# A new order for every step of a long-convolution and soft-MoE kernel on one core

## The chip, the cores and the metric

The kernel runs on one core of one Trainium2 chip, as a single launch. The metric is the time of that core on the device, in microseconds; lower is better. Everything is fp32.

## The reference

Two blocks stand behind each other. The first is a causal long convolution of 8 sequences of 5696 positions and 128 channels with one filter, written as a product of spectra:

```python
Xf = np.fft.rfft(x, n=2 * S, axis=1)
Hf = np.fft.rfft(h, n=2 * S, axis=0)
y = np.fft.irfft(Xf * Hf[None], n=2 * S, axis=1)[:, :S, :]
```

The second takes the 45568 rows of y as tokens of a soft mixture of experts with 32 slots (8 experts of 4):

```python
logits = x @ phi                        # 45568 x 32
d = softmax(logits, over the tokens)    # dispatch
c = softmax(logits, over the slots)     # combine
slot_in = d.T @ x                       # 32 x 128
slot_out[e] = relu(slot_in[e] @ w1[e]) @ w2[e]
out = c @ slot_out
```

So the dispatch needs all tokens before a slot is known, and the output needs the slots.

## The kernel before

The convolution is done as a transform in two factors, 90 x 64, with tables in place of an FFT's twiddles. The filter is group g = 0, the sequences are g = 1 to 8. One `while` loop over steps t (lines 430 to 504) carries everything; each step does one piece of four stages, and the order in which the loop body calls them is the order on each engine, since the schedule is manual.

- **A** (`stage_a`, line 158) transforms one chunk of 4 + 4 positions: `load_x` (135) fetches the low part xl and the mirrored high part xh by four DMAs, `fold` (149) makes their sum xe and difference xo on GpSimd (POOL), TensorE multiplies each with two tables (L165), ScalarE (ACT) copies the banks to fst (L167), and one DMA for each half writes f to HBM. Eight chunks make a group.
- **B** works on units of two frequency pairs, 23 units to a group, three to a step. `load_g` (176) reads gt from f by two DMAs. `stage_b1` (188): the forward product with wt (L195), then on VectorE (DVE) pr and pi, products with the filter's spectrum (L213), and yf, two combinations of them (L217, L219). `stage_b2` (223): the backward product with vt (L231), the copy zst (L234) and two DMAs to z. For the filter's own group DVE and ACT make Hr and Hi instead.
- **C** works on chunks again: `load_z` (248) reads zc; `stage_c1` (259) does four matmuls (L264), a copy yo, and a sum and a difference that are the tokens y (L270, L271); `stage_c2` transposes y (L281), `stage_c3` makes the logits L (L289), column and row maxima cm and rm, and the combine weights ct (POOL, ACT, then the row sums rs on DVE, L306 to L308, POOL again); `stage_c4` transposes ct (L318) and stores it as c_t.
- **Windows** of two chunks carry the running maximum of the dispatch softmax: `window_max` (328) makes c on DVE (L331), transposes it (L335) and reduces it, `window_row` (350) spreads it over the rows (L353) and makes d on POOL and ACT, `dispatch` (371) multiplies d with y into ap and sp (L382, L385), and DVE adds these to acc (L395).

A group's A takes steps 8g to 8g + 7; its B follows 9 steps behind, C 17 steps behind that. So there are steps with A alone, A and B, A and B and C, B and C, and C alone. Before the last stage the buffers of A and B are closed and the expert weights w1s and w2s loaded into their place (line 493). Behind the loop come the expert matmuls (L536, L541) and the output (L564), which multiplies each chunk of c_t with the slots and writes out by two DMAs for each half.

All matmul outputs take turns in six PSUM banks. Nearly all DMAs are issued by SyncE (SP), in the order of the code, and each waits there for its data. An fp32 matmul shows as two MATMUL in the profile.

Of the kernel before, what the change touches and what calls it, by code (L numbers as in the profile page):

```python
# [17 lines left out]
def transform_tables(S, N1, N2):  # L18

    N, R1, HALF = N1 * N2, S // N2, N2 // 2
    k1 = np.arange(N1)
    alpha = np.pi * (k1 + 0.5) / N1
    m1 = np.arange(R1) - (N1 - 1) / 2
    a1 = np.outer(m1, alpha)
    s1 = np.stack([np.cos(a1), -np.sin(a1), -np.cos(a1)], 1)
    i1 = np.stack([np.cos(a1.T), -np.sin(a1.T), -np.cos(a1.T)], 1)  # L30
# [22 lines left out]
def kernel(  # L53
# [44 lines left out]
    zd = [nc.dram_tensor(f"z_{b}", (N1, N2, 2, D), F32, kind="Internal").ap() for b in range(B)]  # L98
# [36 lines left out]
    def load_x(c):  # L135
        if c >= (B + 1) * NJ:
            return
        g, j = divmod(c, NJ)
        src = (h if g == 0 else x[g - 1]).rearrange("(a n) d -> a n d", n=N2)
        xl = apool.tile([R1, CH, D], F32, name="xl", tag="xl")  # L140
        xh = apool.tile([R1, CH, D], F32, name="xh", tag="xh")
        for t_, n0 in ((xl, CH * j), (xh, N2 - CH * (j + 1))):
            for r in (slice(0, SPLIT), slice(SPLIT, R1)):
                nc.sync.dma_start(out=t_[r, :, :], in_=src[r, n0:n0 + CH, :])
        xs[c] = (xl, xh)
# [3 lines left out]
    def fold(c):  # L149
        xl, xh = xs.pop(c)  # L150
        xe = apool.tile([R1, CH, D], F32, name="xe", tag="xe")
        xo = apool.tile([R1, CH, D], F32, name="xo", tag="xo")
        nc.gpsimd.tensor_tensor(out=xe[:, :, :], in0=xl[:, :, :], in1=xh[:, ::-1, :], op=AL.add)  # L153
        nc.gpsimd.tensor_tensor(out=xo[:, :, :], in0=xl[:, :, :], in1=xh[:, ::-1, :],
                                op=AL.subtract)
        folded[c] = (xe, xo)

    def stage_a(c, comp):
        g, j = divmod(c, NJ)
        src = folded[c][comp]  # L160
# [27 lines left out]
    def stage_b1(u):  # L188
# [8 lines left out]
        if g == 0:  # L197
            for q in range(n):
                m = 2 * i + q
                pr = bpool.tile([P, 2, D], F32, name="hp", tag="hp")  # L200
# [22 lines left out]
    def stage_b2(u):  # L223
# [20 lines left out]
    NYB = 5  # L244
# [3 lines left out]
    def load_z(c):  # L248
        if c >= B * NJ:
            return  # L250
        b, j = divmod(c, NJ)
        t_ = cpool.tile([N1, 2, CH, 2, D], F32, name="zc", tag="zc")
        v = zd[b].rearrange("k (o n) c d -> k o (n c d)", o=2)
# [31 lines left out]
    def stage_c3(c):  # L285
# [5 lines left out]
        L = ypool.tile([R1, 2 * CH, NSL], F32, name="L", tag="L", bufs=5)  # L291
# [12 lines left out]
        nc.scalar.activation(ct[:, :, :], ct[:, :, :], AF.Exp)  # L304
        rs = cpool.tile([R1, 2 * CH], F32, name="rs", tag="rs")
# [6 lines left out]
        cs[c] = ct  # L312
# [15 lines left out]
    def window_max(w):  # L328
# [4 lines left out]
                                in1=cm[:, 1:2, :].broadcast_to([R1, Q, NSL]), op=AL.max)  # L333
        p = bank()
# [65 lines left out]
    LAG_B, LAG_C = NJ + 1, 2 * (NJ + 1)  # L400
    PER = -(-NU // NJ)

    def units(t):
        s = t - LAG_B
        g, i = divmod(s, NJ)
        if s < 0 or g > B:
            return []
        return [g * NU + k for k in range(i * PER, min((i + 1) * PER, NU))]

    nc.sync.dma_start(out=s1[:, :, :], in_=t_s1)  # L410
    load_x(0)
# [3 lines left out]
    for p0 in range(0, NP, 9):  # L415
        nc.scalar.dma_start(out=wt[:, p0:p0 + 9, :], in_=t_w[:, p0:p0 + 9, :])
    for p0 in range(0, NP, 9):
        nc.scalar.dma_start(out=vt[:, p0:p0 + 9, :], in_=t_v[:, p0:p0 + 9, :])
    NA, NC = (B + 1) * NJ, B * NJ
    AHEAD = 3  # L420
    queue = [u for t in range(NA + LAG_C + NC) for u in units(t)]
    loaded = 0

    def c_first(t):
        c = t - LAG_C - NJ
        return c if 0 <= c < NC else None

    last_front = max(t for t in range(NA + LAG_C + NC) if units(t))
    t = 0
    while t <= NC + LAG_C + NJ + WC:  # L430
        a = t if t < NA else None
        us = units(t)
        c = c_first(t)
        cp = c_first(t - 1)
        if a is not None:
            load_x(a + 1)
            fold(a)
        if us or units(t + 1):
            pos = queue.index(us[-1]) + 1 if us else 0
            ahead = min(len(queue), pos + AHEAD)  # L440
        else:
            pos = ahead = 0
        nxt = c_first(t + 1)
        if nxt is not None:
            load_z(nxt)

        def want(u):
            nonlocal loaded
            k = min(len(queue), queue.index(u) + 1 + AHEAD)
            while loaded < k and queue[loaded] // NU * NJ + NJ <= t:  # L450
                load_g(queue[loaded])
                loaded += 1

        def b1(k):
            if k < len(us):
                stage_b1(us[k])

        def b2(k):
            if k < len(us):
                stage_b2(us[k])  # L460

        if not us and units(t + 1):
            want(units(t + 1)[0])
        for u in us:
            want(u)
        if a is not None:
            stage_a(a, 0)
        w_row = (c_first(t - WC) or 0) // WC if c_first(t - WC) is not None and c_first(t - WC) % WC == 0 else None
        if c is not None:
            stage_c1(c)  # L470
        if w_row is not None:
            window_row(w_row)
        b1(0)
        if a is not None:
            stage_a(a, 1)
            folded.pop(a)
        if c is not None:
            stage_c2(c)
        b2(0)
        b1(1)  # L480
        if c is not None:
            stage_c3(c)
        dc = c_first(t - WC)
        if dc is not None:
            dispatch(dc)
        b2(1)
        b1(2)
        if cp is not None:
            stage_c4(cp)
        if c is not None and c % WC == WC - 1:  # L490
            window_max(c // WC)
        b2(2)
        if t == last_front:
# [8 lines left out]
            hTz = wts.tile([P, E, NFC, NSL], F32, name="hTz")  # L502
            nc.gpsimd.memset(hTz[:, :, :, :], 0.0)
        t += 1
    assert not (ys or Ls or ds or cs or prods or gs or zs)
# [25 lines left out]
    sop = aps.tile([P, 512], F32, name="ap", tag="ap")  # L531
    for e in range(E):
# [5 lines left out]
        nc.scalar.activation(hTz[:, e, :, e * SPE:(e + 1) * SPE], hv, AF.Relu)  # L538
    for e in range(E):
        for k in range(NFC):  # L540
            nc.tensor.matmul(sop[0:NSL, 0:D], hTz[:, e, k, :], w2s[:, e, k, :],  # L541
                             start=(e == 0 and k == 0), stop=(e == E - 1 and k == NFC - 1))
    so = tail.tile([NSL, D], F32, name="so")
    nc.vector.tensor_copy(out=so[:, :], in_=sop[0:NSL, 0:D])
# [15 lines left out]
    for c in range(B * NJ):  # L560
        b, j = divmod(c, NJ)
        for f in range(2):
# [4 lines left out]
            o_ = osp.tile([R1, CH, D], F32, name="o", tag="o")  # L567
            pv = p[0:R1, :].rearrange("p (n d) -> p n d", d=D)
            if f:
                nc.vector.tensor_copy(out=o_[:, :, :], in_=pv)  # L570
            else:
                nc.scalar.activation(o_[:, :, :], pv, AF.Copy)
            n0 = N2 - CH * (j + 1) if f else CH * j
            for r in (slice(0, SPLIT), slice(SPLIT, R1)):
                nc.sync.dma_start(out=ov[b, r, n0:n0 + CH, :], in_=o_[r, :, :])
# [29 lines left out]
```

## Time and profile before

| | |
|---|---|
| median of 3 runs | 2017.19 us (2013.24 to 2018.6) |
| the profiled execution | 2011.97 us, of it 2010.2 us span |
| TensorE matmul busy | 1671.1 us, 83% |
| DVE, ACT, POOL busy | 753.0, 525.4, 308.6 us |
| mean granted TensorE clock | 0.788 |
| DMA | 277.60 MB, 138 GB/s |

The profile is of one execution. A row of a timeline gives start, length, engine, line, operation, output and inputs, count, and in brackets the idle time ahead of it and what ended it. "PE" is TensorE, "PEld" its weight loads, "SPq" the DMA issues on SP. The granted clock is the share of TensorE's full clock that its throttle let through.

### The profile page before, as it was taken

The numbers are of one execution on the slowest core, as the hardware profiler recorded it, in microseconds if no ns is written. First come the engines' busy times: TensorE is split into PE (matmuls) and PEld (weight loads), VectorE is DVE, ScalarE is ACT, GpSimd is POOL, SyncE is SP. The second block draws the span as 40 slices with busy tenths as digits, with TensorE's granted clock in tenths as the row PEclk, the third lists the DMA queues.
The fourth block names the chain that finished last, engine by engine and source line by source line (L and its number), as shares of the span: only waits on it lengthen the run. The fifth ranks groups of instructions, "written<-read, shape, count | busy, mean of one in ns | idle before, by whom it ended". The sixth has DMA issues, their size and how long they took to land.

```text
span 2010.2 us, 18430 instructions
## 1 busy us (share of the span) xinstructions
PE 1671.1 (83%) x5407; PEld 922.1 (46%) x5407; DVE 753.0 (37%) x1705; ACT 525.4 (26%) x1118; POOL 308.6 (15%) x345
## 2 busy tenths in 40 slices
PE   6986677888888888888888898889878884888999
PEld 2343334444444444444444444444445552445733
DVE  0143434443444344434444434343444531221133
ACT  2462222222222222222222222222221220111133
POOL 2321111111111111111112111111110110110000
PEclk9996878777887788778878878787887875555799
DMA  6675556555555455555555555555453446113166
GB/s 225 187 228 147 153 132 172 139 133 131 141 140 132 129 143 140 132 129 144 140 130 140 142 133 133 136 143 133 125 131 92 108 101 185 40 48 122 49 210 208
DMA packets 204438, 277.60 MB, mean 138 GB/s; under 512 B 24304, under 2 KB 139939, under 8 KB 204339
## 3 DMA queue, kind: packets, MB, share of 16 engines
q1 hardware_dynamic: 202506, 270.36, 50.1%
q10 hardware_dynamic: 1833, 6.06, 0.8%
q8 instruction: 45, 0.74, 0.2%
q14 instruction: 54, 0.44, 0.1%
HBM read 146.89 MB, written 129.43 MB: 137 GB/s over the span
## 4 chain that ended last, share of the span: by engine, by line
PE 66%; DVE 22%; DMA 3%; SPq 3%; POOL 2%; issue 2%; ACT 1%; POOLq 0%; ACTq 0%; DVEq 0%
PE bank L264 18%; PE bank L165 14%; PE bank L231 9%; PE bank L195 8%; PE bank L564 5%; PE ap L382 4%; DVE pr L213 4%; DVE pi L213 4%; DVE yf L217 4%; DVE yf L219 3%; PE bank L289 3%; DVE acc L395 2%; PE bank L536 1%; PE bank L281 1%; POOL ct L301 1%
## 5 line engine op out<-in xcount | busy, mean ns | idle before, releaser
L264 PE MATMUL bank<-zc,i 90*89 90x512 f32 x512 | 384.7, 921 | 21.5 <-DMA zc<-z 21.5
L231 PE MATMUL bank<-yf,vt 128*128 128x256 f32 x720 | 228.1, 444 | 138.6 <-DVE yf L219 138.5
L270 DVE TENSOR_TENSOR y<-bank,yo 89x512 f32<-89x512 f32 x64 | 43.9, 686 | 592.6 <-PE bank L264 541.9
L195 PE MATMUL bank<-gt,wt 128*128 128x256 f32 x810 | 255.3, 446 | 0.0
L165 PE MATMUL bank<-xe,s 89*90 89x512 f32 x288 | 218.4, 903 | 40.6 <-POOL xe L153 40.4
L167 ACT ACTIVATE fst<-bank 90x512 f32<-90x512 f32 x288 | 167.3, 592 | 306.4 <-PE bank L165 259.6
L264 PEld LDWEIGHTS bank<-zc,i 90*89 90x89 f32 x512 | 120.9, 238 | 256.6 <-issue 249.2
L213 DVE TENSOR_TENSOR pr<-bank,Hr 128x512 f32<-128x512 f32 (+1 forms) x184 | 124.4, 676 | 254.6 <-PE bank L195 254.5
L231 PEld LDWEIGHTS bank<-yf,vt 128*128 128x128 f32 x720 | 138.9, 215 | 176.1 <-issue 124.6
L195 PEld LDWEIGHTS bank<-gt,wt 128*128 128x128 f32 x810 | 182.3, 229 | 67.9 <-issue 36.0
L234 ACT ACTIVATE zst<-bank 128x512 f32<-128x512 f32 (+1 forms) x184 | 108.1, 588 | 374.9 <-PE bank L231 329.4
L165 PE MATMUL bank<-xo,s 89*90 89x512 f32 x288 | 177.6, 750 | 0.0
L382 PE MATMUL ap<-y,d 89*128 89x512 f32 x256 | 164.9, 735 | 1.5 <-ACT d L366 1.5
L301 POOL TENSOR_TENSOR ct<-L,rm 89x256 f32<-89x256 f32 x64 | 39.2, 612 | 776.1 <-DVE rm L299 776.1
L153 POOL TENSOR_TENSOR xe<-xl,xh 89x512 f32<-89x512 f32 x72 | 90.7, 1259 | 231.1 <-DMA xh<-in_x_dram 180.9
L213 DVE TENSOR_TENSOR pi<-bank,Hi 128x512 f32<-128x512 f32 (+1 forms) x184 | 123.0, 669 | 0.0
L165 PEld LDWEIGHTS bank<-xe,s 89*90 89x90 f32 x288 | 61.7, 220 | 130.4 <-issue 64.2
L564 PE MATMUL bank<-sobd,cT 128*89 128x512 f32 x256 | 111.8, 600 | 2.5 <-DVE sobd L555 2.5
L289 PEld LDWEIGHTS bank<-phi,yt 128*89 128x89 f32 x1024 | 104.0, 179 | 13.3 <-ACT yt L282 7.8
L363 POOL TENSOR_TENSOR d<-L,mr 89x256 f32<-89x256 f32 x64 | 45.1, 724 | 422.5 <-DVE mr L355 422.5
L289 PE MATMUL bank<-phi,yt 128*89 128x32 f32 x1024 | 102.3, 257 | 5.8 <-ACT yt L282 5.8
L335 PE MATMUL bank<-ident,c 89*128 89x89 f32 x32 | 11.0, 342 | 111.3 <-DVE c L331 111.3
(74 smaller groups left out, 1445.4 us busy)
## 6 DMA issues: line engine op xcount, KB each, us to landing
f<-fst SPq DMA_DIRECT2D x144, 360.0 KB, 3.6
gt<-f SPq DMA_DIRECT2D x396, 128.0 KB, 5.0
zc<-z SPq DMA_DIRECT2D x64, 720.0 KB, 6.3
z<-zst SPq DMA_DIRECT2D x352, 128.0 KB, 2.5
out_dram<-o SPq DMA_DIRECT2D x128, 160.0 KB, 2.2
xl<-in_x_dram SPq DMA_DIRECT2D x64, 160.0 KB, 2.5
xh<-in_x_dram SPq DMA_DIRECT2D x64, 160.0 KB, 2.5
c_t<-cst SPq DMA_DIRECT2D x64, 89.0 KB, 1.6
```

The lines of the kernel that those rows point to most:

```text
L153: nc.gpsimd.tensor_tensor(out=xe[:, :, :], in0=xl[:, :, :], in1=xh[:, ::-1, :], op=AL.add)
L165: nc.tensor.matmul(p[0:N1, :], s1[:, tab[G], :], src[:, :, :].rearrange("p n d -> p (n d)"), start=True, stop=True)
L167: nc.scalar.activation(st[:, :, G, :], p[0:N1, :].rearrange("p (n d) -> p n d", d=D), AF.Copy)
L195: nc.tensor.matmul(p[:, q * 256:(q + 1) * 256], wt[:, 2 * i + q, :], t_[:, q, :, :].rearrange("p c d -> p (c d)"), start=True, stop=True)
L213: nc.vector.tensor_tensor(out=t[:, 0:n, :, :], in0=pv[:, 0:n, :, :], in1=H[:, 2 * i:2 * i + n, :].unsqueeze(2).broadcast_to([P, n, 2, D]), ...
L217: nc.vector.tensor_tensor(out=y_[:, 0:n, 0, :], in0=pr[:, 0:n, 0, :], in1=pi[:, 0:n, 1, :], op=AL.subtract)
L231: nc.tensor.matmul(p[:, q * 256:(q + 1) * 256], vt[:, 2 * i + q, :], y_[:, q, :, :].rearrange("p c d -> p (c d)"), start=True, stop=True)
L234: nc.scalar.activation(st[:, 0:n, :], p[:, 0:n * 256].rearrange("p (q c) -> p q c", q=n), AF.Copy)
L264: nc.tensor.matmul(p[0:R1, :], i1[:, tabs[q], :], t_[:, o, :, q, :], start=(q == 0), stop=(q == 1))
L289: nc.tensor.matmul(p[0:R1, i * NSL:(i + 1) * NSL], yt[:, i, :], phi[:, :], start=True, stop=True)
L382: nc.tensor.matmul(ap_[:, :], dv, y_[:, f * CH:(f + 1) * CH, :].rearrange("p n d -> p (n d)"), start=first, stop=last)
L564: nc.tensor.matmul(p[0:R1, :], cT[:, c, f, :], sobd[:, f, :, :].rearrange("p q d -> p (q d)"), start=True, stop=True)
```

## The change

The stages are the same but for the three below; their order and their distance are new. A `for` loop takes the place of the `while` loop:

```diff
+        def slot_b():
+            nonlocal loaded
+            if us:
+                u = us.pop(0)
+                while loaded < len(queue) and queue[loaded][0] <= u + AHEAD \
+                        and queue[loaded][0] // NU * NJ + NJ <= t:
+                    load_g(queue[loaded][0])
+                    loaded += 1
+                stage_b1(u)
+                wait_b2.append(u)
+                if len(wait_b2) > 1:
+                    stage_b2(wait_b2.pop(0))
+            elif wait_b2:
+                stage_b2(wait_b2.pop(0))
...
+        c = chunk(0)
+        if chunk(-1) is not None:
+            load_z(chunk(-1))
+        if t < NA:
+            load_x(t + 3)
+            stage_a(t, 0)
+            fold(t + 1, 0)
+        r = chunk(3)
+        if r is not None and r % WC == 0:
+            window_row(r // WC)
+        slot_b()
+        c1 = chunk(1)
+        if c1 is not None:
+            stage_c2(c1)
         if c is not None:
             stage_c1(c)
...
+        slot_b()
+        if c1 is not None:
+            stage_c3(c1)
+        if t < NA:
+            stage_a(t, 1)
+            fold(t + 1, 1)
+        slot_b()
+        if c1 is not None:
+            stage_c3b(c1)
+            if c1 % WC == WC - 1:
+                window_max(c1 // WC)
+        if chunk(2) is not None:
+            stage_c4(chunk(2))
+        if c1 is not None and c1 % WC == WC - 1:
+            window_top(c1 // WC)
+        if r is not None:
+            dispatch(r)
```

`chunk(lag)` is the chunk whose C1 was `lag` steps ago: C1 stands at 0, C2 and C3 at 1, C4 at 2, the window's row and the dispatch at 3. `stage_c3b` is the second part of the old `stage_c3`, from the row sums rs on; `window_top` is the old `window_max` from its transpose on. In a slot the forward product of unit u stands ahead of the backward product of unit u - 1. `AHEAD` goes from 3 to 4 units, x is loaded three chunks ahead in one tile xc of three buffers, and folded one chunk ahead. The buffers of y and of L go from 5 to 4.

Three kinds of transfers are merged. Both parts of x come by one access pattern (two DMAs for four), z is stored by one DMA for a unit (two before; its layout in HBM changes, and the rows of the table i1 with it), and the two halves of an output chunk share their DMAs (two for four):

```diff
+        t_ = apool.tile([R1, 2, CH, D], F32, name="xc", tag="xc", bufs=3)
...
-        for par in range(2):
-            k0 = par * NP + 2 * i
-            nc.sync.dma_start(
-                out=zd[g - 1][k0:k0 + n, :, :, :].rearrange("k r c d -> r k (c d)"),
-                in_=st[par * N2:(par + 1) * N2, 0:n, :])
+        nc.sync.dma_start(
+            out=zd[g - 1][2 * i:2 * i + n, :, :, :].rearrange("q r c d -> r q (c d)"),
+            in_=st[:, 0:n, :])
```

The tables wt and vt were loaded by ACT's queue at the start; now SP loads a seventh of wt in each of steps 2 to 8, and of vt in each of steps 9 to 15. The expert weights are loaded one step later. The second expert product takes w2s as the stationary operand:

```diff
-            nc.tensor.matmul(sop[0:NSL, 0:D], hTz[:, e, k, :], w2s[:, e, k, :],
-                             start=(e == 0 and k == 0), stop=(e == E - 1 and k == NFC - 1))
+            for e in range(e0, e0 + 4):
+                nc.tensor.matmul(pp[e - e0][:, 0:SPE], w2s[:, e, k, :], hT[:, e, k, :],
+                                 start=(k == 0), stop=(k == NFC - 1))
```

and a transpose (with 8 small copies on DVE) turns the slots back.

What stands on the engines, in a step with A, B and C that ends a window. TensorE before, from the third stage of a chunk to the first of the next (phi: C3; ap and sp: dispatch; ct: C4; c: the window's transpose; gt and yf: B; xe and s: A; zc: C1):

```order
L289 MATMUL bank<-phi,yt 89x32 x8
L382 MATMUL ap<-y_100,d 128x512
L385 MATMUL sp<-ones,d 128x1
L382 MATMUL ap<-y_100,d 128x512
L385 MATMUL sp<-ones,d 128x1
L231 MATMUL bank<-yf,vt 128x256 x2
L195 MATMUL bank<-gt,wt 128x256 x2
L318 MATMUL bank<-ident,ct 128x89 x2
L335 MATMUL bank<-ident,c_4743 128x89
L231 MATMUL bank<-yf,vt 128x256 x2
L165 MATMUL bank<-xe,s_92 90x512 x2
L264 MATMUL bank<-zc,i_68 89x512 x4
```

And TensorE after, from C1 on (x_4447: the second half of A):

```order
L265 MATMUL bank<-zc,i_68 89x512 x4
L198 MATMUL bank<-gt,wt 128x256 x2
L234 MATMUL bank<-yf,vt 128x256 x2
L290 MATMUL bank<-phi,yt 89x32 x8
L168 MATMUL bank<-x_4447,s_92 90x512 x2
L198 MATMUL bank<-gt,wt 128x256 x2
L234 MATMUL bank<-yf,vt 128x256 x2
L322 MATMUL bank<-ident,ct 128x89 x2
L343 MATMUL bank<-ident,c_4612 128x89
L390 MATMUL ap<-y_99,d 128x512
L393 MATMUL sp<-ones,d 128x1
```

A forward and a backward product, of different units, now stand side by side; the dispatch went behind the window's transpose, and the second half of A between C3 and the third slot.

DVE before, ahead of the window's c:

```order
L296 TENSOR_REDUCE cm_104<-L 89x32
L299 TENSOR_REDUCE rm<-L 89x8
L306 TENSOR_REDUCE rs<-ct 89x8
L307 TENSOR_SCALAR rs<-rs 89x8
L308 RECIPROCAL rs<-rs 89x8
L395 SCALAR_TENSOR_TENSOR acc<-acc,dn,ap 32x128 x4
L395 SCALAR_TENSOR_TENSOR acc<-acc,dn,sp 128x1
L213 TENSOR_TENSOR pr<-bank,Hr 128x512
L213 TENSOR_TENSOR pi<-bank,Hi 128x512
L217 TENSOR_TENSOR yf<-pr,pi 128x2x128
L219 TENSOR_TENSOR yf<-pr,pi 128x2x128
L331 TENSOR_TENSOR c_4743<-cm_104 89x128
```

DVE after, at the same place:

```order
L297 TENSOR_REDUCE cm_103<-L 89x32
L300 TENSOR_REDUCE rm<-L 89x8
L216 TENSOR_TENSOR pr<-bank,Hr 128x512
L216 TENSOR_TENSOR pi<-bank,Hi 128x512
L220 TENSOR_TENSOR yf<-pr,pi 128x2x128
L222 TENSOR_TENSOR yf<-pr,pi 128x2x128
L311 TENSOR_REDUCE rs<-ct 89x8
L312 TENSOR_SCALAR rs<-rs 89x8
L313 RECIPROCAL rs<-rs 89x8
L335 TENSOR_TENSOR c_4612<-cm_103 89x128
```

The third unit's products and the row sums have changed places, both still ahead of c; the sums into acc went behind it.

SP before, one step of DMA issues:

```order
L255 DMA zc<-z 90x2x1024
L183 DMA gt<-f 64x512 x6
L170 DMA f<-fst 90x4x256 x2
L238 DMA z<-zst 64x2x256 x4
L323 DMA c_t<-cst 128x178
L238 DMA z<-zst 64x2x256 x2
L144 DMA xl<-in_x_dram 80x512
L144 DMA xl<-in_x_dram 9x512
L144 DMA xh<-in_x_dram 80x512
L144 DMA xh<-in_x_dram 9x512
```

SP after, the same:

```order
L256 DMA zc<-z 90x2x1024
L147 DMA xc<-in_x_dram 80x2x512
L147 DMA xc<-in_x_dram 9x2x512
L173 DMA f<-fst 90x4x256
L186 DMA gt<-f 64x512 x2
L239 DMA z<-zst 128x2x256
L186 DMA gt<-f 64x512 x2
L239 DMA z<-zst 128x2x256
L173 DMA f<-fst 90x4x256
L186 DMA gt<-f 64x512 x2
L239 DMA z<-zst 128x2x256
L327 DMA c_t<-cst 128x178
```

The 20 issues of a step are 15, and the reads of gt stand between the writes of f and z.

More of the change, by code (lines that the diff above doesn't have):

```diff
@@ L29, in transform_tables @@
     s1 = np.stack([np.cos(a1), -np.sin(a1), -np.cos(a1)], 1)
-    i1 = np.stack([np.cos(a1.T), -np.sin(a1.T), -np.cos(a1.T)], 1)
+    rows = np.arange(N1).reshape(2, N1 // 2).T.reshape(-1)
+    i1 = np.stack([np.cos(a1.T), -np.sin(a1.T), -np.cos(a1.T)], 1)[rows]
     k2 = np.arange(N2)
@@ L97 @@
     fd = [nc.dram_tensor(f"f_{g}", (N2, N1, 2, D), F32, kind="Internal").ap() for g in range(B + 1)]
-    zd = [nc.dram_tensor(f"z_{b}", (N1, N2, 2, D), F32, kind="Internal").ap() for b in range(B)]
+    zd = [nc.dram_tensor(f"z_{b}", (NP, 2 * N2, 2, D), F32, kind="Internal").ap() for b in range(B)]
     cd = nc.dram_tensor("c_t", (P, B * NJ, 2, R1), F32, kind="Internal").ap()
@@ L333, in window_max, with window_top @@
                                 in1=cm[:, 1:2, :].broadcast_to([R1, Q, NSL]), op=AL.max)
+        mrows[w] = c4
+    def window_top(w):
+        c4 = mrows[w]
         p = bank()
@@ L397, in dispatch @@
                                                op0=AL.mult, op1=AL.add)
-    LAG_B, LAG_C = NJ + 1, 2 * (NJ + 1)
+    LAG_B, LAG_C = NJ + 1, 3 * NJ + 2
     PER = -(-NU // NJ)
+    NA, NC = (B + 1) * NJ, B * NJ
     def units(t):
-        s = t - LAG_B
-        g, i = divmod(s, NJ)
-        if s < 0 or g > B:
+        g, i = divmod(t - LAG_B, NJ)
+        if t < LAG_B or g > B:
             return []
         return [g * NU + k for k in range(i * PER, min((i + 1) * PER, NU))]
+    steps = NC + LAG_C + WC + 2
+    queue = [(u, t) for t in range(steps) for u in units(t)]
+    last_front = queue[-1][1] + 1
+    AHEAD = 4
+    loaded = 0
     nc.sync.dma_start(out=s1[:, :, :], in_=t_s1)
-    load_x(0)
+    for c in range(3):
+        load_x(c)
     nc.scalar.dma_start(out=phi[:, :], in_=moe_phi)
@@ L414 @@
     nc.scalar.dma_start(out=i1[:, :, :], in_=t_i1)
[L415 to L447, printed above, removed]
-            nonlocal loaded
[L449 to L468, printed above, removed]
@@ new lines, with chunk @@
+    for comp in range(2):
+        fold(0, comp)
+    wait_b2 = []
+    for t in range(steps):
+        us = list(units(t))
+        def chunk(lag):
+            c = t - LAG_C - lag
+            return c if 0 <= c < NC else None
+        def slot_b():
+            nonlocal loaded
+            if us:
[10 more added lines that the diff above has]
+                stage_b2(wait_b2.pop(0))
+        if t < NJ + 1 and t >= 2:
+            p0 = NP * (t - 2) // (NJ - 1)
+            p1 = NP * (t - 1) // (NJ - 1)
+            nc.sync.dma_start(out=wt[:, p0:p1, :], in_=t_w[:, p0:p1, :])
+        if NJ + 1 <= t < 2 * NJ:
+            p0 = NP * (t - NJ - 1) // (NJ - 1)
+            p1 = NP * (t - NJ) // (NJ - 1)
+            nc.sync.dma_start(out=vt[:, p0:p1, :], in_=t_v[:, p0:p1, :])
+        c = chunk(0)
[12 more added lines that the diff above has]
+            stage_c2(c1)
@@ L469 @@
         if c is not None:
             stage_c1(c)
[L471 to L489, printed above, removed]
@@ L501 @@
                                   in_=moe_w2[e].rearrange("(c p) d -> p c d", p=P))
[L502 to L505, printed above, removed]
+    assert not (ys or Ls or ds or cs or prods or gs or zs or xs or folded or wait_b2)
     tail = work.enter_context(tc.tile_pool(name="tail", bufs=1))
@@ L537 @@
                              siT[:, e * SPE:(e + 1) * SPE], start=True, stop=True)
-        nc.scalar.activation(hTz[:, e, :, e * SPE:(e + 1) * SPE], hv, AF.Relu)
-    for e in range(E):
+        nc.scalar.activation(hT[:, e, :, :], hv, AF.Relu)
+    soT = tail.tile([P, NSL], F32, name="soT")
+    for e0 in range(0, E, 4):
+        pp = [bank() for _ in range(4)]
         for k in range(NFC):
-            nc.tensor.matmul(sop[0:NSL, 0:D], hTz[:, e, k, :], w2s[:, e, k, :],
-                             start=(e == 0 and k == 0), stop=(e == E - 1 and k == NFC - 1))
+            for e in range(e0, e0 + 4):
+                nc.tensor.matmul(pp[e - e0][:, 0:SPE], w2s[:, e, k, :], hT[:, e, k, :],
+                                 start=(k == 0), stop=(k == NFC - 1))
+        for e in range(e0, e0 + 4):
+            nc.vector.tensor_copy(out=soT[:, e * SPE:(e + 1) * SPE], in_=pp[e - e0][:, 0:SPE])
+    p = bank()
+    nc.tensor.transpose(p[0:NSL, 0:D], soT[:, :], ident[:, :])
     so = tail.tile([NSL, D], F32, name="so")
-    nc.vector.tensor_copy(out=so[:, :], in_=sop[0:NSL, 0:D])
+    nc.vector.tensor_copy(out=so[:, :], in_=p[0:NSL, 0:D])
     rep2 = tail.tile([NSL, Q, NSL], F32, name="rep2")
```

63 lines of the change are left out of this document (33 added, 30 removed).

## Prediction

> **What bounds the kernel now.** I read the page first, then the waits of TensorE, then a table by stage, then the timeline of single steps. In this page PE is TensorE's matmuls, and PEclk is the clock that the throttle granted in each fortieth of the span, in tenths:
>
> ```profile
> span 2010.2 us, 18430 instructions
> ...
> PE 1671.1 (83%) x5407; PEld 922.1 (46%) x5407; DVE 753.0 (37%) x1705; ACT 525.4 (26%) x1118; POOL 308.6 (15%) x345
> ...
> PEclk9996878777887788778878878787887875555799
> ```
>
> TensorE is busy for 83% of the span, no other engine for half of it, so the time is TensorE's. But its clock is rarely whole: a good part of the 1671 us is slow work, not much work. The same by stage (0 to 12 is the first load); the columns are busy time of each engine, then PEclk, the busy share of the DMA engines, GB/s:
>
> ```profile
> 12.00:80.00 68.00, 62.69 (x72) 18.72 (x72) 0.00 (x0) 21.40 (x36) 22.41 (x19) 1.00 0.66 212
> 80.00:145.00 65.00, 55.07 (x155) 29.40 (x155) 26.18 (x88) 41.58 (x121) 20.24 (x18) 0.95 0.77 227
> 145.00:307.00 162.00, 113.10 (x275) 62.45 (x276) 65.13 (x106) 36.42 (x64) 24.77 (x19) 0.77 0.56 152
> 307.00:1461.00 1154.00, 980.50 (x3395) 549.70 (x3394) 487.58 (x1099) 315.57 (x657) 200.65 (x226) 0.80 0.53 137
> 1461.00:1650.00 189.00, 156.13 (x583) 100.18 (x582) 85.69 (x209) 41.53 (x93) 18.06 (x28) 0.78 0.44 105
> 1650.00:1846.00 196.00, 147.55 (x417) 77.85 (x415) 42.58 (x130) 28.38 (x72) 20.73 (x30) 0.53 0.32 90
> 1846.00:1894.00 48.00, 44.38 (x260) 43.16 (x261) 1.96 (x10) 2.65 (x12) 0.00 (x0) 0.67 0.19 78
> 1894.00:2010.00 116.00, 111.69 (x256) 40.65 (x256) 43.92 (x64) 37.90 (x64) 0.00 (x0) 0.98 0.65 202
> ```
>
> I call them stages 1 to 8: A alone; A with the filter's B; A and B (9 steps); A, B and C (46 steps, 25.1 us each); B and C (9 steps); C alone; the expert matmuls; the output. Stage 4 decides. What TensorE waits for, over the whole trace (us, times, longest):
>
> ```profile
> PE bank L231 <- DVE yf L219: 138.5, 71, 4.5
> PE bank L335 <- DVE c L331: 111.3, 32, 4.6
> PE bank L165 <- POOL xe L153: 40.4, 14, 12.4
> PE bank L264 <- DMA zc<-z: 21.5, 1, 21.5
> ```
>
> So two waits on DVE matter: the backward product on its products yf, and the window's transpose on c. Here is one step of stage 4 on TensorE (start, us, and in brackets the idle time before it), and one group from the step ahead of it:
>
> ```profile
> 1112.66 7.03 PE L264 MATMUL bank<-zc,i 90*89 90x512 f32 x8
> ...
> 1135.78 1.10 PE L231 MATMUL bank<-yf,vt 128*128 128x256 f32 x4 [3.52 <-DVE yf L219]
> 1136.72 1.88 PE L165 MATMUL bank<-xe,s 89*90 89x512 f32 x4
> 1138.44 3.60 PE L264 MATMUL bank<-zc,i 90*89 90x512 f32 x8
> 1141.87 1.03 PE L195 MATMUL bank<-gt,wt 128*128 128x256 f32 x4
> 1142.74 1.88 PE L165 MATMUL bank<-xo,s 89*90 89x512 f32 x4
> ...
> 1147.36 1.38 PE L289 MATMUL bank<-phi,yt 128*89 128x32 f32 x16
> 1148.58 1.10 PE L382 MATMUL ap<-y,d 89*128 89x512 f32 x2
> ...
> 1152.55 0.32 PE L318 MATMUL bank<-ident,ct 89*128 89x89 f32 x2
> 1156.75 0.27 PE L335 MATMUL bank<-ident,c 89*128 89x89 f32 x1 [3.88 <-DVE c L331]
> 1156.85 1.06 PE L231 MATMUL bank<-yf,vt 128*128 128x256 f32 x4
> ```
>
> The same eight L264 take 7.03 us in one step and 3.60 in the next: half clock and whole. A gap therefore costs twice, once as idle time and once as the slow work behind it. When the clock falls and when it comes back (columns: TensorE busy, PEclk, DMA):
>
> ```profile
> 1134.00:1137.40 3.40, 1.62 (x6) 1.00 0.24 57
> 1154.50:1157.90 3.40, 1.15 (x6) 1.00 0.27 64
> 1157.90:1161.30 3.40, 3.40 (x6) 0.50 0.40 85
> ...
> 1663.00:1878.00 215.00, 169.20 (x519) 103.55 (x520) 38.99 (x122) 26.83 (x72) 17.71 (x27) 0.50 0.28 85
> ```
>
> A stretch of 3.4 us with 1.62 us of matmul kept the clock, one with 1.15 lost it. And in stage 6, with 169 of 215 us busy, it stayed at 0.50 throughout: there the dense matmuls feed 89 or 90 rows (L264, L382). In stage 8, whose L564 feeds 128 rows, it is 0.98. So I take it that the clock falls after about 3.4 us less than some 40% busy, and returns after about 3.4 us that are dense and hold some 128-row work (L195, L231).
>
> **The change part by part.**
>
> *Stage 4, the dense work.* No matmul is added or taken away. From 1136.72 to the end of L318 (1152.55 + 0.2) are 16.0 us at whole clock, without the third L231 group, which stands behind the gap: 0.94 (1135.78 to 1136.72). Sum 16.9, with a short wait in it and three units, where a chunk has 23 in eight steps. The other way: 980.5 us x 0.80 = 784, / 46 = 17.05. I take 16.8, 773 us for 46 steps.
>
> DVE in that same step:
>
> ```profile
> 1142.14 0.69 DVE L270 TENSOR_TENSOR y<-bank,yo 89x512 f32<-89x512 f32 x1 [6.51 <-PE bank L264]
> ...
> 1143.35 0.68 DVE L213 TENSOR_TENSOR pr<-bank,Hr 128x512 f32<-128x512 f32 x1
> ...
> 1145.00 0.42 DVE L219 TENSOR_TENSOR yf<-pr,pi 128x256 f32<-128x256 f32 x1
> ...
> 1151.74 0.42 DVE L306 TENSOR_REDUCE rs<-ct 89x8 f32<-89x256 f32 x1 [1.26 <-ACT ct L304]
> ...
> 1152.39 0.20 DVE L308 RECIPROCAL rs<-rs 89x8 f32<-89x8 f32 x1
> ...
> 1156.33 0.28 DVE L331 TENSOR_TENSOR c<-cm 89x128 f32<-89x128 f32 x1
> ```
>
> *The waits on yf go.* A unit's products take DVE 2.07 us (1143.35 to 1145.42). Now the backward product of unit u stands behind the forward one of u+1, and between the two slots lie C2 and C1, or C3 and A, or the dispatch and A: at least 1.22 + 1.72 us (starts of L289 and L382; of L165 and L264). With the 0.87 us of L195 (1141.87 to 1142.74) and 0.94 of L231 that is 4.7 us from the end of a unit's L195 to its L231, against 2.07 plus what stands ahead on DVE, at most the two y (1.21). Nothing for the wait is left. The other end is that a wait of today's mean length, 138.5 / 71 = 2.0 us, comes back in each step; it is kept for the range.
>
> *The wait on c stays, shorter.* In the new order c stands on DVE behind the third unit and the row sums. Count from the end of C1 (T = 1141.87 here). TensorE: two groups of B, 1.81; C3 1.22; A 1.72; two groups of B, 1.81; two transposes 0.2: it is at the window's transpose at T + 6.75. DVE: the third forward product ends at T + 5.6, its products start 0.27 later (as y does behind C1, 1142.14 - 1141.87) and end at T + 7.95; the three rs take 0.85 (1151.74 to 1152.59); from the start of c to L335 were 0.42. That is T + 9.2. The gap is 2.4 us in every second step, against 111.3 / 32 = 3.5 now. Bounds: 1.6 if the row sums come ahead of the products in time, 3.5 as now.
>
> *What the clock then does.* A stretch of 3.4 us around a gap of 2.4 is under 1.15 us busy when it holds nearly all of the gap, and over 1.62 when it holds less than about 1.8: between half and five sixths of the gaps should drop the clock. Behind the gap come the dispatch (1148.58 to 1152.55 less the two B groups in it, 2.16 us) and A (1.72), no 128-row work, then B, which restores it: some 8 us at half, 4 lost. I take 3.0 us for a gap on average (1.5 to 4).
>
> *Sum of stage 4:* 773 + 23 x 2.4 + 23 x 3.0 + 0.2 a step for the rest = 906 us, so -248. The DMA engines move the same bytes: 0.53 x 1154 = 612 us of their time, a share of 0.68, and stage 2 shows 0.77. SP gets fewer issues (15 for 20 in a step). Behind SP's in-order waits on the copies of A stand the gt loads, four units ahead now, and the next zc, a whole step ahead; neither is near its use.
>
> *Stage 3.* TensorE's work at whole clock is 113.10 x 0.77 = 87 us, the DMA engines' 0.56 x 162 = 91 us. At the share of stage 2, 0.77, it would be 118, at 1.0 it is 91. I take 110: -52 (-68 to -30).
>
> *Stage 5.* 156.13 x 0.78 = 122 at whole clock; without A the transpose is reached 1.72 earlier, DVE is ready no more than that earlier, so the gap is between 2.4 and 4.1; 2.8 taken, since DVE's queue is short there, and 2.6 for the clock (B is nearer): 4.5 x 5.4 = 24, so 146, -43 (-50 to -20).
>
> *Stages 1 and 2.* Of the waits on xe (40.4 in all) I count half here, and they go, since x is loaded three chunks and folded one ahead. But the first gt are now asked for only in the slot that uses them, and the tables wt and vt move from ACT's queue at the start into SP's, into stages 1 and 2 with their 0.66 and 0.77: I let that take back 15 of the 20, so -5 (-12 to +5).
>
> *Stage 6.* 89- and 90-row work stays at half clock. The weight loads stand ahead of a zc as now, so its 21.5 us stay. Of the other idle time (196 - 147.55 - 21.5 = 27) I take a quarter away: -7 (-15 to +5).
>
> *Stages 7 and 8.* The second expert product loads w2s as weights instead of hTz:
>
> ```profile
> L536 PE MATMUL bank<-siT,w1s 128*128 128x4 f32 x128 | 27.5, 354 | 0.3 <-DVE siT L530 0.3
> ...
> L541 PE MATMUL ap<-w2s,hTz 128*32 128x128 f32 x128 | 16.1, 295 | 0.0
> ```
>
> 128 instructions of L536's form for 128 of L541's: +11.4, and eight small copies and a transpose behind them, +2: +13 (+8 to +15; the low end if the clock is whole). The output stays with TensorE (111.69 of 116); it starts at half clock now, since the 128-column L541 ahead of it is gone: +1. Merged output transfers lie under it.
>
> Total: -248 - 52 - 43 - 5 - 7 + 13 + 1 = -341; span 1669, its own time (2011.97 for 2010.2 now) 1671. That execution was 5.2 us under the median of the runs (2017.19), so **1676**.
>
> **The rivals.**
>
> *The gap no longer drops the clock.* Then the 23 x 3.0 and 4.5 x 2.6 go: 1595. For it: a gap of 3.52 us at 1132 to 1136 left the clock whole. Against: 1.15 busy of 3.4 dropped it, and a gap of 2.4 can do that. The Trainium skill's page "TensorE: Matmul & The Clock Gate" (section "Why this matters for your kernels") asks only that idle gaps stay under about 3 us, and by that rule this rival is the forecast. Its Part 1 lets any sustained busy window restore the clock; the 215 us of stage 6 disagree.
>
> *A new wait in the even steps too.* On ACT the exponential of ct, which waits for DVE and POOL, now stands ahead of the copies of A's second half, which free the banks. If that makes a gap in each step, stage 4 costs 16.8 + 2.4 + 3.0 + 0.2 = 22.4 a step, 1030: with stage 5 about 1800. Against: six banks last until the next step's A.
>
> *Transfers set the pace.* If the DMA engines can't pass the 0.56 and 0.53 that stages 3 and 4 show, these two keep their time: 1976. Against: 0.77 in stage 2.
>
> *Slower: the clock stays at half.* If B's groups, cut into single slots among 90-row work, never make a stretch dense enough, stage 4 is at 0.50 as stage 6: 784 x 2 = 1568 instead of 1154, and with stages 3 and 5 (174 and 244) the total is near 2500. It decides from a mean clock in stage 4 below about 0.66 (784 / 0.66 + 55 is 1154 plus the 93 won elsewhere). Against: each slot holds 1.81 us of 128-row work, 3.6 at half clock.
>
> **How the numbers follow.** Forecast 0.55 (1625 to 1735 by its own bounds), no drop of the clock 0.18, a gap in each step 0.19, transfers 0.05, slower 0.03. The range 1580 to 1800 holds the first two and half of the third. A measurement of this kernel tells about 0.3% from no change; all cases but the last are far on the fast side: faster 0.96, same 0.01, slower 0.03.
>
> **What would show it.** Right: L231 waits for yf under 20 us in all; the window's transpose waits for c 32 times at 2.4 to 2.8 us; PEclk in stage 4 of 0.88 to 0.94 and steps of 19 to 20.5 us; stage 7 longer by 11 us or more. Wrong: a new first wait of TensorE on ACT, POOL or a transfer; PEclk at or under 0.8 in stage 4; a DMA share over 0.85 with TensorE idle.

## The result and the profile after

The changed kernel takes 1585.24 us in the median of four runs (1577.03 to 1594.1), the kernel before 2016.84: a ratio of 0.786 (95% interval 0.782 to 0.791). The profiled execution took 1586.2 us, its span is 1584.1. One of the four executions of a later experiment (the 128-row filler in stage 6) took 2643 us, far from its other three, and is left out of every number here. The page of the changed kernel, the same lines as before:

```profile
span 1584.1 us, 17798 instructions
...
PE 1451.1 (92%) x5408; PEld 864.3 (55%) x5408; DVE 712.0 (45%) x1713; ACT 510.6 (32%) x1118; POOL 305.3 (19%) x344
...
PEclk9989999898889998999898899898998555555999
```

TensorE is busy for 220 us less with nearly the same work (5408 matmuls for 5407), so it works faster. Its table by stage (busy time of each engine, PEclk, DMA share, GB/s):

```profile
12.00:74.00 62.00, 61.89 (x73) 20.25 (x74) 0.00 (x0) 20.86 (x36) 22.71 (x19) 1.00 0.71 200
74.00:148.00 74.00, 59.84 (x154) 31.57 (x153) 25.54 (x86) 40.80 (x117) 20.24 (x16) 0.88 0.82 237
148.00:237.00 89.00, 80.54 (x286) 50.45 (x284) 53.91 (x110) 37.88 (x67) 25.32 (x20) 1.00 0.88 264
237.00:1080.00 843.00, 800.24 (x3356) 494.17 (x3357) 454.87 (x1085) 300.20 (x652) 196.69 (x223) 0.93 0.67 188
1080.00:1219.00 139.00, 125.71 (x591) 86.18 (x590) 86.34 (x217) 39.15 (x93) 16.70 (x26) 0.90 0.54 148
1219.00:1408.00 189.00, 155.00 (x441) 85.50 (x440) 44.33 (x137) 29.78 (x77) 21.59 (x33) 0.50 0.34 100
1408.00:1467.00 59.00, 55.96 (x259) 55.29 (x259) 2.83 (x18) 2.38 (x11) 0.00 (x0) 0.50 0.07 30
1467.00:1584.00 117.00, 111.89 (x256) 40.89 (x256) 44.17 (x65) 38.22 (x65) 0.00 (x0) 0.98 0.68 200
```

Counted from the first A or C1 of a stage's first step to that of the next, which is finer than the windows of the two tables, stage 1 is 6 us shorter, 2 is 10 longer, 3 is 75 shorter, 4 is 309, 5 is 51, 6 is 7, 7 is 12 longer, 8 less than one.

The clock of 1.00 in stage 1 is no measurement, here and in the table of before: the trace's records of the clock begin only at 88.6 us (86.1 before). At the end of this stage 21 matmuls of 512 columns (L168) take 18.13 us, 0.86 each; in stage 4 eight of that width (L265) take 3.60 us at whole clock, 0.43 each from start to start. So stage 1 runs at half clock.

What TensorE still waits for:

```profile
PE bank L343 <- DVE c L335: 72.5, 32, 3.4
PE bank L198 <- DMA gt<-f: 14.8, 5, 5.8
PE bank L168 <- POOL x L157: 12.1, 1, 12.1
PE bank L265 <- DMA zc<-z: 12.0, 2, 11.5
PE bank L234 <- DVE yf L222: 7.4, 11, 1.4
```

The wait on yf went from 138.5 us to 7.4, that on c from 111.3 to 72.5. The second one still does this, in a step of stage 4 that ends a window:

```profile
903.77 1.93 PE L168 MATMUL bank<-x,s 89*90 89x512 f32 x4
905.54 1.03 PE L198 MATMUL bank<-gt,wt 128*128 128x256 f32 x4
906.41 1.03 PE L234 MATMUL bank<-yf,vt 128*128 128x256 f32 x4
907.27 0.32 PE L322 MATMUL bank<-ident,ct 89*128 89x89 f32 x2
909.67 0.30 PE L343 MATMUL bank<-ident,c 89*128 89x89 f32 x1 [2.08 <-DVE c L335]
...
912.59 3.70 PE L168 MATMUL bank<-x,s 89*90 89x512 f32 x4
```

A gap of 2.08 us, and behind it the four L168 take 3.70 us where four of them took 1.93 before it: the clock fell.

### The profile page after: what moved, and what is told of

Same layout as the page of the kernel before. It is cut to its first block, busy times and chain, and to the rows that moved or that the text cites. A ratio compares the mean times of both kernels' runs of the same rounds, so it can differ in the third digit from the quotient of the medians.

```text
span 1584.1 us, 17798 instructions
## 1 busy us (share of the span) xinstructions
PE 1451.1 (92%) x5408; PEld 864.3 (55%) x5408; DVE 712.0 (45%) x1713; ACT 510.6 (32%) x1118; POOL 305.3 (19%) x344
## 4 chain that ended last, share of the span: by engine, by line
PE 85%; DVE 7%; DMA 4%; issue 2%; ACT 1%; POOL 1%; SPq 0%; POOLq 0%; DVEq 0%
PE bank L168 19%; PE bank L265 16%; PE bank L198 11%; PE ap L390 9%; PE bank L234 8%; PE bank L573 7%; PE bank L290 5%; PE bank L282 3%; PE bank L537 2%; PE bank L545 2%; DMA gt<-f 2%; DVE pr L216 1%; DVE pi L216 1%; DMA zc<-z 1%; PE sp L393 1%
## 5 line engine op out<-in xcount | busy, mean ns | idle before, releaser
L168 PE MATMUL bank<-x,s 89*90 89x512 f32 x576 | 335.0, 719 | 12.2 <-POOL x L157 12.1
L265 PE MATMUL bank<-zc,i 90*89 90x512 f32 x512 | 262.9, 661 | 12.0 <-DMA zc<-z 12.0
L198 PE MATMUL bank<-gt,wt 128*128 128x256 f32 x810 | 232.5, 413 | 15.3 <-DMA gt<-f 14.8
L157 POOL TENSOR_TENSOR x<-xc 89x512 f32<-89x512 f32 x144 | 182.5, 1268 | 318.5 <-PE bank L168 261.4
L234 PE MATMUL bank<-yf,vt 128*128 128x256 f32 x720 | 195.2, 394 | 7.4 <-DVE yf L222 7.4
L168 PEld LDWEIGHTS bank<-x,s 89*90 89x90 f32 x576 | 100.7, 188 | 138.3 <-issue 106.9
L265 PEld LDWEIGHTS bank<-zc,i 90*89 90x89 f32 x512 | 83.5, 174 | 136.6 <-issue 116.9
L393 PEld LDWEIGHTS sp<-ones,d 89*128 89x128 f32 x256 | 62.2, 243 | 85.0 <-issue 85.0
L220 DVE TENSOR_TENSOR yf<-pr,pi 128x256 f32<-128x256 f32 (+1 forms) x184 | 79.3, 431 | 6.4
L573 PEld LDWEIGHTS bank<-sobd,cT 128*89 128x89 f32 x256 | 40.9, 160 | 72.8 <-issue 72.5
```

What stands on the lines that cost most here:

```text
L157: nc.gpsimd.tensor_tensor(out=y_[:, :, :], in0=t_[:, 0, :, :], in1=t_[:, 1, ::-1, :], op=AL.subtract if comp else AL.add)
L168: nc.tensor.matmul(p[0:N1, :], s1[:, tab[G], :], src[:, :, :].rearrange("p n d -> p (n d)"), start=True, stop=True)
L198: nc.tensor.matmul(p[:, q * 256:(q + 1) * 256], wt[:, 2 * i + q, :], t_[:, q, :, :].rearrange("p c d -> p (c d)"), start=True, stop=True)
L220: nc.vector.tensor_tensor(out=y_[:, 0:n, 0, :], in0=pr[:, 0:n, 0, :], in1=pi[:, 0:n, 1, :], op=AL.subtract)
L234: nc.tensor.matmul(p[:, q * 256:(q + 1) * 256], vt[:, 2 * i + q, :], y_[:, q, :, :].rearrange("p c d -> p (c d)"), start=True, stop=True)
L265: nc.tensor.matmul(p[0:R1, :], i1[:, tabs[q], :], t_[:, o, :, q, :], start=(q == 0), stop=(q == 1))
```

## The experiments

Each line here is a kernel of its own; the details follow. Each ratio (with its 95% interval) is to runs of the kernel before on the same chip. The last four columns are the stages 2 to 5 of its profile in us, each from the first A or C1 of its first step to that of the next stage.

| kernel | median us | ratio to before | 2 | 3 | 4 | 5 |
|---|---|---|---|---|---|---|
| before | 2017 | 1 | 65 | 164 | 1152 | 190 |
| before + one behind | 1818 | 0.900 (0.898-0.903) | 65 | 105 | 1053 | 150 |
| before + one behind + folds ahead | 1702 | 0.847 (0.843-0.852) | 62 | 109 | 941 | 151 |
| changed | 1585 | 0.786 (0.782-0.791) | 75 | 89 | 843 | 138 |
| changed, backward first | 1685 | 0.840 (0.835-0.844) | 71 | 122 | 896 | 155 |
| changed, transfers split | 1610 | 0.796 (0.793-0.800) | 73 | 101 | 852 | 148 |
| changed, gap filled | 1513 | 0.749 (0.747-0.751) | 74 | 91 | 789 | 126 |
| changed, c early | 1452 | 0.720 (0.718-0.722) | 71 | 89 | 738 | 123 |
| best | 1394 | 0.691 (0.689-0.693) | 70 | 89 | 738 | 129 |

**c early.** `window_max` is called in another place:

```diff
             stage_c3(c1)
+            if c1 % WC == WC - 1:
+                window_max(c1 // WC)
...
             stage_c3b(c1)
-            if c1 % WC == WC - 1:
-                window_max(c1 // WC)
```

> The changed kernel with one move: the window's maximum c goes on VectorE right behind the column and row maxima, ahead of the third unit's products. Theory (the wait on c is what still drops the clock): the 72.5 us of waits on c go to under 10, the granted clock in the stage with A, B and C goes from 0.93 to 0.98 or more, that stage from 843 to about 760, the one with B and C from 139 to about 122, the one with C alone loses its 3.4 us gaps: 1465 us in all (1445 to 1490). Rival (the clock falls for other reasons, only idle time counts): at most the 72.5 us of waiting are won, 1513 or more, with the clock still near 0.93.

1452.47 us (1449.76 to 1456.21). What is left of the waits on c, and its stages 4 and 5:

```profile
PE bank L343 <- DVE c L335: 8.0, 7, 1.3
...
234.00:972.00 738.00, 737.00 (x3363) 463.73 (x3362) 462.42 (x1085) 298.67 (x653) 196.97 (x223) 1.00 0.75 214
972.00:1095.00 123.00, 116.49 (x585) 80.64 (x584) 87.28 (x217) 38.22 (x93) 16.80 (x27) 0.97 0.58 162
```

TensorE is busy for 737 of 738 us at whole clock: 16.04 us a step is the dense work. 133 us are won where the waits on c fell by 64.5 us (72.5 to 8.0), so the rest was the clock. The theory holds.

**Gap filled.**

```diff
+            if t < last_front:
+                p = bank()
+                for _ in range(5):
+                    nc.tensor.matmul(p[:, 0:256], vt[:, 0, :],
+                                     Hr[:, 0:2, :].rearrange("p m d -> p (m d)"),
+                                     start=True, stop=True)
             window_top(c1 // WC)
```

> The changed kernel with work added: ahead of the window's transpose TensorE does five useless 128-row products of 256 columns (2.15 us at whole clock, 27 times, 58 us in all) in the stages that have B. Nothing is moved. Theory (the clock falls because the gap leaves a stretch under-used): the clock goes to 0.98 or more there, the waits on c shrink to about the 10 late windows, and although TensorE does 58 us more the time falls by 40 to 65, to 1520 to 1545. Rival (idle time alone counts): the filler takes the place of the idle time and runs past it, the same time or up to 20 us more.

1512.66 us (1509.33 to 1515.53). Stage 4:

```profile
239.00:1028.00 789.00, 788.31 (x3581) 504.08 (x3582) 457.71 (x1084) 298.33 (x653) 196.55 (x223) 1.00 0.71 200
```

More matmuls (3581 for 3356 in this stage), and 54 us less: the clock is 1.00 for 0.93. Nothing was moved, so this shows the price of the clock by itself. The gain (73 us in all) is a little over what was expected (40 to 65); the waits on c are 19.0 us.

**Before, one behind.** The first part of the change alone, in the kernel before:

```diff
-        b2(0)
         b1(1)
+        b2(0)
...
-        b2(1)
         b1(2)
+        b2(1)
```

with the third backward product of a step moved behind the next step's first forward one.

> The kernel before with one part of the change: each backward product stands behind the next unit's forward product (the last one of a group excepted). Stages of C, folds and loads are where they were. Theory (the waits on the products yf were half of the idle time and brought the clock down behind them): these waits go from 138.5 to under 20 us, the wait on c stays and grows to about 4 us each, the stage with A, B and C goes from 1154 to about 975, all in all 1750 us (1700 to 1810). Rival (the lag of C's stages is what pays): other waits take their place and less than 100 us are won, 1915 or more.

1818.15 us (1813.98 to 1820.57), just past the theory's range:

```profile
PE bank L335 <- DVE c L331: 102.4, 32, 5.5
PE bank L165 <- POOL xe L153: 75.4, 38, 12.4
PE bank L264 <- DMA zc<-z: 21.3, 1, 21.3
PE bank L231 <- DVE yf L219: 11.8, 14, 2.4
```

The waits on yf went from 138.5 to 11.8 and some 200 us were won, but the waits on xe rose from 40.4 to 75.4: a wait took part of the place of the one removed. So stage 4 took 1053 us and not the 975 expected. The waits on c did not grow, as the theory had it, but fell from 111.3 to 102.4.

**Before, one behind, folds ahead.** On top of that, `load_x(a + 2)` for `load_x(a + 1)` and `fold(a + 1)` behind the second half of A for `fold(a)` at the step's start.

> The kernel before with two parts of the change: the backward product behind the next forward one (1818 us by itself), and x loaded and folded one chunk further ahead. Theory (the waits on xe that came up in the first were the folds' place): the waits on xe go from 75 to under 25 us, those on c stay at 3 to 5 us each, 1720 in all (1690 to 1750); what is then left to the changed kernel is the lag of C's stages. Rival (the folds only moved the wait): the time of c or yf grows by as much, 1800 or more.

1702.18 us (1694.42 to 1708.15). The theory holds: the waits on xe are 13.2 us, those on c 93.9 (2.9 each, 3 to 5 said). By the ratios (each to the kernel before on its own chip), some 200 of the 432 us belong to the product one behind, 107 to x loaded and folded further ahead, and the other 123 to what is left, each good to about 10 us. What is left is above all the lag of C's stages, the merged transfers, and the expert product, which costs; no run has the lag alone, so its share is not shown. The lag means this: C1 stands where it stood, 18 steps behind the A of its own group and 9 behind its B (17 only behind the filter's B), while C2, C3, C4 and the dispatch come one step later than before.

**Backward first.**

```diff
+                if wait_b2:
+                    stage_b2(wait_b2.pop(0))
                 stage_b1(u)
                 wait_b2.append(u)
-                if len(wait_b2) > 1:
-                    stage_b2(wait_b2.pop(0))
```

> The changed kernel with the two products of a slot swapped: the backward product of the last unit stands ahead of the next unit's forward product, so that only the work between two slots covers a unit's 2.07 us on VectorE. Theory (any 2.7 us between the slots would do): no loss where A, B and C run, since at least 2.9 us lie between; a wait of some 2.6 us a step where only A and B run (nothing lies between the first two slots) and of 1.4 where only B and C run: 1620 in all (1605 to 1640). Rival (standing behind the next forward product is what pays everywhere): a wait of 2 us or more in each step with A, B and C too, 1680 or more.

1684.63 us (1681.15 to 1693.73): the rival's number, but not by its mechanism. Where only A and B run, the waits on yf are 26.4 us, 2.9 a step, and where only B and C run 7.4, about as the theory had it; these two stages lose 33 and 17 us. The waits of stage 4 alone:

```profile
PE bank L343 <- DVE c L335: 49.9, 17, 2.9
PE bank L343 <- ACT zst L237: 7.7, 5, 1.6
PE bank L265 <- PE bank L282: 6.5, 8, 0.8
PE bank L234 <- DVE yf L222: 1.7, 3, 0.6
```

There is next to no wait on yf where A, B and C run (1.7 us), as the theory had it. But the third forward product now ends one group later, so c comes that much later: gaps up to 2.9 us where the changed kernel has 2.1, a clock of 0.90 for 0.93, 53 us more in this stage. Each gap on c is a lever on the clock.

**Transfers split.** x by a DMA for each part, z by one for each half of the partitions, the output by one for each half.

> The changed kernel with its merged transfers split again: x by four transfers a chunk, z by two a unit, the output by four a chunk (five issues more in a step). Theory (transfers lie under the matmuls): within 0.5 per cent, 1577 to 1593. Rival (fewer issues are part of the gain): 1600 or more, with a new wait of TensorE on gt, zc or x.

1609.5 us (1597.29 to 1613.97). The rival is right in part: merging is worth about 1.3%, and the waits on gt rise from 14.8 to 22.1 us, 9.9 us of the 22.1 in stage 3. 12 us of the loss lie in stage 3, which sits at a DMA share of 0.80 instead of 0.88, the rest in stages 4 and 5. Split transfers also keep the DMA engines busy for longer: 0.70 x 852 = 596 us in stage 4, for 0.67 x 843 = 565. Why each split transfer costs more than its issue was not tried.

**Stage 6 woken.** On top of c early, in the eight steps with C alone, between C2 and C1:

```diff
+        if c is not None and t > last_front:
+            p = bank()
+            for _ in range(2):
+                nc.tensor.matmul(p[:, :], ones[0:128, :], junk[0:128, :],
+                                 start=True, stop=True)
```

> The version with c moved early (1452 us), with useless work added in the eight steps with C alone: two 128-row products of 512 columns a step, between C2 and C1 (1.7 us at whole clock). Theory (the clock is restored by dense work that feeds all 128 rows): these steps, at half clock until now, go to whole clock, 10 to 11 us each for 17.7, and the time falls to 1410 (1395 to 1428) although 14 us of work are added. Rival (any dense work would have restored it, and something else holds the clock at half there): no change of the clock, 27 us more.

> The same as the version with 128-row products in the steps with C alone, but these products feed 89 rows only; they last as long. Theory (rows count, not busy time): the clock stays at half, and the 8 times 3.4 us come on top, 1475 (1465 to 1485). Rival (busy time counts): the same time as with 128 rows.

(The second kernel has 89 in place of 128.) With 128 rows 1434.62 us (1430.42 to 1439.5), with 89 rows 1475.68 (1468.29 to 1479.67), against 1452.47 without. As ratios to the kernel before these are 0.7145 (0.7105-0.7184), 0.734 (0.7297-0.7383) and 0.7195 (0.7176-0.7215): in the total the two fillers differ clearly, while the intervals of the 128 rows and of no filler touch. The stage itself shows that gain. The first C1 to the last of this stage, without filler and then with 128 rows:

```profile
1095.00:1236.00 141.00, 121.60 (x346) 66.56 (x346) 34.41 (x98) 23.45 (x60) 15.51 (x24) 0.50 0.39 107
...
1097.00:1219.00 122.00, 100.80 (x380) 55.32 (x379) 35.51 (x102) 24.38 (x64) 16.86 (x26) 0.74 0.45 124
```

and with 89:

```profile
1101.00:1259.00 158.00, 136.68 (x387) 71.87 (x385) 36.29 (x104) 24.69 (x64) 16.85 (x26) 0.55 0.35 95
```

The same number of columns, as dense; only the rows differ. 128 rows bring the clock back, 89 do not (0.55 holds the first 16 us of the stage, still at whole clock). The theory of the first misses its size, 1435 for 1410: in the timeline of those steps the clock falls again at each window's gap of 1.5 us and comes back only with the next step's filler, some 8 us later.

**Stage 2.** Two kernels for the 10 us that stage 2 lost: the first five gt a step earlier (`load_g(0)` to `load_g(4)` in step 8), and wt and vt back on ACT's queue at the start.

> The changed kernel, with the first five gt of the filter's group asked for one step earlier, in the last step with A alone. Theory (the steps with A and the filter's B are longer than before, 75 us for 65, since the first gt are late): the first wait of 5.8 us on gt goes, these steps take 68 to 70 us, 1579 in all (1572 to 1588). Rival (the tables wt and vt in the same steps fill the DMA engines): the waits on gt only move, 74 us stay.

> The changed kernel, with the tables wt and vt loaded by ScalarE's queue at the start, as before. Theory (late first gt): the 75 us stay, the steps with A alone get longer by the 5 to 10 us that the tables take from x, 1592 in all (1585 to 1600). Rival (the tables fill the DMA engines in the steps with A and the filter's B): these steps fall to 65 to 68 us, and what the first steps lose is less: 1575 to 1585.

1578.91 us (1574.4 to 1582.15) and 1583.72 (1580.79 to 1588.64); stage 2 takes 69 and 67 us for 75, and starts at 74 us, as in the changed kernel, and at 77. Both causes are there: the gt account for 6 us, the tables for 7, of which they take 3 back ahead of it. In the total, 0.4% and nothing that can be told from no change.

**Best.** c early, the first gt early, the second expert product in its old form, and the 128-row filler in the first nine steps and ahead of the window's transpose in stage 6.

> What the runs point to, together: the changed kernel with c moved early, the first gt asked for a step earlier, the second expert product in its old form (w2s streams past hTz), and useless 128-row products (two of 512 columns) in the first nine steps and ahead of the window's transpose in the steps with C alone. Theory: 1452 less 12 for the expert product, 5 for gt, 30 for the clock in the steps with C alone and 5 to 10 in those with A alone: 1400 (1380 to 1420). Rival (the pieces take each other's place, above all the first steps held by transfers): 1425 or more.

1393.95 us (1391.26 to 1396.96), 12% under the changed kernel and inside the theory's range. Stage 4 is as with c early alone. Stage 1 is 13 us shorter than in the changed kernel: behind the first filler, eight of its matmuls take 3.60 us.

## Why the prediction was right, point by point

The time lies at the low end of the range (1580), under the forecast's own bounds (1625 to 1735) and 91 us under its number (1676). That it is in the range is in part luck: the range reached so low for the sake of a rival (1595) whose mechanism the runs reject. The direction and the mechanism held; three sizes were off.

- **The waits on yf go:** right, 7.4 us (under 20 said). The experiment with one behind alone shows them to be worth some 200 us with their clock.
- **The wait on c stays, shorter:** right, 32 times, 2.3 us on average, just under the 2.4 to 2.8 said, and 1.9 in stage 4.
- **The clock falls at that gap:** right. Stage 4 has 843 - 738 - 43 = 62 us of it (738 dense from c early, 43 waits), 2.7 a gap where 3.0 was taken. By the trace's records of the clock, 14 of the 22 gaps there dropped it (between half and five sixths said): 14 of the 17 of about 2.08 us, and none of the five of 1.46. The rival with a clock that no longer falls had the nearest number, 1595, and is wrong: filling the gap won 73 us. The Trainium skill's "TensorE: Matmul & The Clock Gate" (section "Why this matters for your kernels") warns of idle gaps over about 3 us; here one of 2.08 dropped the clock, so the measurement decides.
- **The dense work of stage 4: too high, and the largest miss.** 773 us said (16.8 a step), 738 measured (16.04). Both ways to it were high. The one step held three units where the mean is 2.875, and a short wait. And busy time was multiplied by the mean clock of the whole stage, although the idle time lay nearly all at whole clock: of 464 us at half clock in the trace of that stage, 454 were busy, so the work was 980 - 227 = 753 us and not 784. The same product was too high in stage 3 (80 for 87) and in stage 5 (117 for 122). The dense work is 35 of the 61 us by which the stage beat its forecast (-309 for -248); the others are the waits on c (55 said, 43 measured), the clock behind them (69 and 62) and the 0.2 a step (9, of which nothing is seen).
- **Stage 3:** 110 said, 89 measured. The DMA engines went to a share of 0.88, not to the 0.77 of stage 2, and TensorE ran at whole clock, busy for 80.5 of the 89 us. A share seen in a stage that waits for something else is no ceiling.
- **Stage 5:** -51 for -43, the dense work again. **Stages 7, 8:** +12 and less than +1 for +13 and +1.
- **Stage 6:** -7 for -7, but by luck. The wait on zc, said to stay at 21.5 us, fell to 11.5; the waits on c rose from 8.6 to 17.0, and the busy time from 148 to 155; other idle time fell by 13.
- **Stages 1 and 2:** +4 for -5. The two costs were named; they took back more than all, and not 15 of 20: where 27 us of waits on xe stood, there are now 12.1 on x and 13.6 on gt, and stage 2 has a clock of 0.88 for 0.95.
- **A new wait in the even steps, transfers as the pace, a clock that stays at half:** none of them came. The waits on ACT come to 2.8 us in the whole trace, PEclk in stage 4 is 0.93 (0.88 to 0.94 said), and a step there takes 18.3 us (19 to 20.5 said). The DMA share, 0.67 for 0.68, agrees by luck: it is 565 us of 843 where 612 of 906 were said.

## What to carry to other kernels

Price a gap of TensorE by the clock of the work behind it, not by its own length: here 64.5 us of waits, once they were gone, gave back 133. When a reordering leaves one wait, look at what stands ahead of its producer in that engine's queue; a single call moved up won a third as much again as the whole change. And take the dense cost of a step from a stretch without gaps at whole clock, with the right count of units, rather than from busy time times a mean clock that also holds the idle time.

## What the runs showed of the hardware

The clock's spells in these traces are whole multiples of 3.41 us, but for the last of each trace. For each such window I added up the streaming time of its matmuls, from the timeline's rows (0.43 us for 512 columns at whole clock, twice that at half), each weighted with the rows it feeds over 128. In the kernel before, all 60 windows behind which the clock fell have 0.362 or less, and all of the more than 200 behind which it stayed 0.378 or more; in the changed kernel the two bounds are 0.348 and 0.378. Without the weight they overlap (0.41 and 0.39 before, 0.50 and 0.41 after). Over the traces of all thirteen kernels the line is less sharp, between 0.36 and 0.40. No window under 0.71 brings the clock back, and every one over 0.77 does; a dense stream of 89 or 90 rows ends at 0.70. This is a fit to these traces. It says that such matmuls hold a whole clock but can't regain one, which is what the pair with 128 and 89 rows shows by experiment. The Trainium skill's "TensorE: Matmul & The Clock Gate" (Part 1) lets any sustained busy window restore the clock; stage 6, 155 of 189 us busy at 0.50, disagrees. So does stage 1, 61.89 of 62 us busy with 89-row work at half clock.
